# The 36 stores of bias rows of an attention and FFN kernel, issued by GpSimd in place of SyncE

## The chip, the cores and the metric

The kernel runs on one core of one Trainium2 chip. The metric is the device time of one execution in microseconds (us); the comparison below is between medians of several executions. Engines are named as the profile names them: PE (TensorE), DVE (VectorE), ACT (ScalarE), POOL (GpSimd) and SP (SyncE). SP does no arithmetic here: it only issues DMA transfers.

## The reference

Attention over 2 batches, 8 heads, 576 positions and 64 dimensions per head, with a position bias that a small network computes, followed by two feed-forward layers over the 1152 tokens:

```python
scores = scale * np.matmul(q, k.transpose(0, 1, 3, 2))
psi_rel = np.log1p(np.abs(pos[:, None] - pos[None, :]).astype(np.float32))
x = (psi_rel / np.log1p(np.maximum(pos[:, None].astype(np.float32), 1.0)))[..., None]
bias = np.maximum(x @ w1 + b1, 0.0) @ w2          # hidden 32, one column per head
attn = softmax(scores + bias.transpose(2, 0, 1)[None])
x = (attn @ v)                                     # to 1152 x 512
h = x @ w_in; x = (h * np.clip(h + 3.0, 0.0, 6.0) / 6.0) @ w_out     # d_ff 2048
xn = x / sqrt(mean(x * x) + 1e-06) * rms_g
out = (silu(xn @ w_gate) * (xn @ w_val)) @ w_out2  # d_ff 1536
```

## The kernel before

**Bias.** The bias is computed in 36 groups of 16 query positions (n = 0 to 35). For each group DVE and ACT build four tiles `R` (L361, L356), PE multiplies them with the second layer's weights into PSUM (`bias_mm`, rows `bps` L374, in the table B.n), ACT or DVE scales the result into a tile `ev` (`bias_evac`, L398 and L396; the pool has four such buffers, so group n+4 in issue order can only be written when the store of its predecessor in that buffer has landed), and `bias_store` (L404) writes it to DRAM: 16 positions x 8 heads x 591 values, in which the relative distances stand in one row. Eight groups make one DRAM buffer `biasd` (five of them, c = 0 to 4; the program calls c = 0, 1, 2, 3, 4 biasd_72, 73, 74, 75, 76). When all stores of a buffer have landed, `bias_load` (L427, L430) reads it back with a skewed pitch, so that each of 128 query rows gets its own 576 columns: tile `bias`, two heads at a time. The first unit's load is cut into its two heads.

**Attention.** It runs over 9 tiles of 128 queries and, in each, 4 pairs of heads: 36 units u. In a unit PE makes the scores `s` (S.u, L445), DVE adds the bias and takes the minimum into `e` (L458, twice, once per head), ACT takes the exponential (L469), PE transposes (T.u.0 to 2, rows `tps`), ACT or DVE copies to `et` (L489), and PE multiplies with v (PV.u, L507). q and k are transposed by PE first (qT, kT, rows `qps` and `kps`) and copied (`kS`, L332 on DVE; `q`, L342 on ACT). PE's order is a table written by hand, which contains among others `B.8 kT.0,0,1 qT.1.0 S.1 T.0.0 B.14 T.0.2 S.2`. The PSUM pool of the transposes has three buffers, that of the scores two. The loads of q (`rawq`, L290), k (`rawk`, L300) and v (`vs`, `v`, L308 and L310) and of the weights (`raw`, L127) are all issued by SP.

**Order.** Only PE's order is fixed by hand there. The other engines, SP among them, get their order when the program is built, from a scheduler with its own estimates; each engine then works strictly in that order. A DMA's semaphore is one of eight of its issuing side in turn, so a ninth DMA waits until the first of the eight has landed.

**POOL** does little in the attention part: the 1/sum rows are spread over a tile (`rb`, L521, which PE transposes as `rps`) and the lower half of the output is split off (`xl`, L543), each once for a tile. In the two feed-forward layers POOL makes the lower parts of the weights (`wl`, L168).

Of the kernel before, what the change touches and what calls it, by code (L numbers as in the profile page):

```python
# [65 lines left out]
def kernel(ctx, tc, q, k, v, w1, b1, w2, w_in, w_out, w_gate, w_val, w_out2, rms_g, dtab, ntab, itab, out):  # L66
    nc = tc.nc
    B, H, S, D = q.shape
# [170 lines left out]
    if True:  # L239
# [123 lines left out]
        ev_t = {}  # L363
# [36 lines left out]
        def bias_store(n):  # L400
            c, m = divmod(n, 8)
            dst = biasd[c][:(128 if c < 4 else 64) * (H + 1) * W].rearrange("(s h w) -> s h w", h=H + 1, w=W)
            lo = S - 16 - 16 * n
            nc.sync.dma_start(out=dst[16 * m:16 * m + 16, :H, lo:lo + S + 15], in_=ev_t.pop(n))  # L404

        def bias_rows(c, p):
            rows = 128 if c < 4 else 64
# [186 lines left out]
        for i, n in enumerate(n for c in order for n in range(8 * c, min(8 * c + 8, NG))):  # L594
            g = group_key(i)
            z = "z" if i < 8 else ""
            R_eng[n] = "".join(sorted(START[i] if i < 8 else MID[i % len(MID)], key="PDA".index))
            for j, x in enumerate(sorted(range(4), key=lambda x: "PAD".index(R_eng[n][x]))):
                e = R_eng[n][x]
                at(g + (P[z + "rp"] if e == "P" else P[z + "ra"] if e == "A" else P[z + "rd"] * j), ("R", n, x), (), bias_R, n, x, e)  # L600
            at(g + P[z + "b"], ("B", n), [("R", n, x) for x in range(4)] + [("cc",)], bias_mm, n)
            o = 16 * n + 15
            for h, length in enumerate((o, S - o)):
                e = "D" if length <= P[z + "evd"] else "A"
                at(g + P[z + "ev"] + .001 * h, ("EV", n, h), [("B", n)], bias_evac, n, h, e)
            key = g + P[z + "ev"] + .001 + P[z + "st"]
            at(key, ("ST", n), [("EV", n, 0), ("EV", n, 1)], bias_store, n)
            c = n // 8
            stored_key[c] = max(stored_key.get(c, -99), key)
# [335 lines left out]
```

## Time and profile before

| what | value |
|---|---|
| median of 3 runs | 646.74 us (646.6 to 648.12) |
| profiled execution, its own time | 646.28 us |
| span of its profile | 644.5 us |
| mean granted TensorE clock | 0.999 |
| PE busy | 622.3 us, 97% of the span |
| DVE, ACT, POOL busy | 461.5, 346.5, 144.5 us |

The span goes from the first to the last instruction; the profiled execution's own time lies 1.8 us above it. A busy share is a share of the whole span, and says little of one stage.

### The profile page before, as it was taken

What the parts mean: (1) busy time and instruction counts of PE and PEld (TensorE: products, weight loads), DVE (VectorE), ACT (ScalarE), POOL (GpSimd) and SP (SyncE); (2) the same over time, 40 slices, a digit from 0 to 9 for tenths busy, and PEclk for the clock granted to TensorE, in tenths of its full rate; (3) what the DMA queues carried; (4) which work ended last, traced back from release to release, by engine and by line L of the source; (5) the groups of instructions that cost most, each with busy time, mean ns of one, the idle gap of its engine ahead of it and who ended that gap; (6) DMA issues with size and microseconds to landing.
All of it is one profiled execution on the core that took longest, in us unless ns stands there. A gap on an engine that the chain in (4) does not pass through costs nothing.

```text
span 644.5 us, 10984 instructions
## 1 busy us (share of the span) xinstructions
PE 622.3 (97%) x4174; PEld 527.5 (82%) x4174; DVE 461.5 (72%) x855; ACT 346.5 (54%) x700; POOL 144.5 (22%) x116
## 2 busy tenths in 40 slices
PE   5889999998999999999999999999999999999997
PEld 2356666676788999999999989999899999999996
DVE  6797788647754999998833799969776761397812
ACT  4878676877765555555534556564444431253511
POOL 1000111011310333333310023323332340032400
PEclk9999999999999999999999999999999999999999
DMA  6999647478600344444310133443434350154301
GB/s 149 289 314 284 174 134 196 112 157 255 200 1 2 95 136 131 131 132 130 119 44 1 35 98 131 134 128 99 148 113 131 102 159 2 34 184 143 99 0 50
DMA packets 74721, 80.16 MB, mean 124 GB/s; under 512 B 23980, under 2 KB 59436, under 8 KB 74668
## 3 DMA queue, kind: packets, MB, share of 16 engines
q1 hardware_dynamic: 74668, 79.46, 41.8%
q8 instruction: 33, 0.54, 0.4%
q14 instruction: 20, 0.16, 0.1%
HBM read 66.19 MB, written 13.25 MB: 123 GB/s over the span
## 4 chain that ended last, share of the span: by engine, by line
PE 88%; DVE 4%; ACT 3%; DMA 3%; issue 1%; SPq 0%; DVEq 0%; ACTq 0%
PE h L735 39%; PE ya L780 18%; PE yb L780 9%; PE pv L507 6%; PE tps L103 5%; PE s L445 5%; PE bps L374 3%; DVE R L361 1%; ACT e L469 1%; ACT ev L398 1%; DMA raw<-in_moe_w_in_dram 1%; DVE e L458 1%; DMA bias<-biasd 1%; PE qps L103 1%; DMA biasd<-ev 1%
## 5 line engine op out<-in xcount | busy, mean ns | idle before, releaser
L168 POOL TENSOR_TENSOR wl<-wm,wh 128x512 fp32r<-128x512 f32 x85 | 126.3, 1486 | 302.4 <-ACT wh L139 183.3
L160 DVE SCALAR_TENSOR_TENSOR wm<-raw,wm 128x512 int32<-128x512 int32 x85 | 121.9, 1434 | 1.0
L744 ACT CAST gh<-r 128x384 fp32r<-128x384 f32 x84 | 43.2, 514 | 115.4 <-DVE r L767 68.6
L735 PE MATMUL h<-nh,wh 128*128 128x384 f32 x288 | 97.3, 338 | 0.0
L735 PE MATMUL h<-nh,wl 128*128 128x384 f32 x288 | 96.7, 336 | 0.0
L735 PE MATMUL h<-nl,wh 128*128 128x384 f32 x288 | 96.4, 335 | 0.0
L469 ACT ACTIVATE e<-e,m 128x576 f32<-128x576 f32 x72 | 55.5, 772 | 31.9 <-DVE m L458 31.7
L735 PE MATMUL h<-xh,wh 128*128 128x384 f32 x192 | 65.4, 341 | 0.0
L767 DVE TENSOR_TENSOR r<-r,h 128x384 f32<-128x384 f32 x36 | 19.9, 553 | 63.0 <-PE h L735 63.0
L735 PE MATMUL h<-xh,wl 128*128 128x384 f32 x192 | 64.7, 337 | 0.0
L735 PE MATMUL h<-xl,wh 128*128 128x384 f32 x192 | 64.4, 336 | 0.0
L156 DVE SCALAR_TENSOR_TENSOR wm<-raw,wm 128x512 int32<-128x512 int32 x85 | 59.4, 698 | 2.8
L458 DVE CUSTOM_DVE_ANT_1 e<-s,bias 128x576 f32<-128x576 f32 x72 | 52.4, 757 | 10.6 <-PE s L445 8.0
L147 ACT ACTIVATE wm<-raw 128x512 f32<-128x512 f32 x85 | 57.2, 673 | 3.5 <-DMA raw<-in_moe_w_in_dram 2.1
L747 DVE TENSOR_TENSOR gl<-r,gh 128x384 fp32r<-128x384 f32 x84 | 46.6, 554 | 16.8 <-ACT gh L744 16.8
L735 PEld LDWEIGHTS h<-nh,wh 128*128 128x128 f32 x288 | 54.1, 188 | 2.3 <-DVE nl L844 0.9
L735 PEld LDWEIGHTS h<-nl,wh 128*128 128x128 f32 x288 | 54.1, 188 | 1.4
L103 PE MATMUL tps<-ident,e 128*128 128x128 f32 x324 | 53.1, 297 | 2.0 <-ACT et L489 1.6
L361 DVE TENSOR_SCALAR R<-T,NB 128x320 f32<-128x320 f32 (+17 forms) x124 | 50.6, 462 | 6.0 <-PE bps L374 5.7
L735 PEld LDWEIGHTS h<-nh,wl 128*128 128x128 f32 x288 | 54.0, 188 | 0.0
L103 PEld LDWEIGHTS tps<-ident,e 128*128 128x128 f32 x324 | 41.5, 201 | 14.6 <-issue 7.3
L755 ACT ACTIVATE r<-h,half_c 128x384 f32<-128x384 f32 x48 | 27.7, 578 | 47.7 <-PE h L735 47.6
(102 smaller groups left out, 1095.8 us busy)
## 6 DMA issues: line engine op xcount, KB each, us to landing
raw<-in_moe_w_out_dram SPq DMA_DIRECT2D x33, 512.0 KB, 3.6
biasd<-ev SPq DMA_DIRECT2D x36, 295.5 KB, 3.7
raw<-in_moe_w_in_dram SPq DMA_DIRECT2D x18, 512.0 KB, 3.6
raw<-in_moe_w_gate_dram SPq DMA_DIRECT2D x18, 512.0 KB, 3.5
bias<-biasd SPq DMA_DIRECT2D x15, 576.0 KB, 4.8
raw<-in_moe_w_val_dram SPq DMA_DIRECT2D x16, 512.0 KB, 3.6
rawq<-in_q_dram SPq DMA_DIRECT2D x32, 128.0 KB, 4.6
bias<-biasd SPq DMA_DIRECT2D x10, 288.0 KB, 4.4
```

Source lines behind the costliest of these rows:

```text
L103: nc.tensor.transpose(out, in_, ident[:n, :n])
L147: nc.scalar.activation(out=m, in_=raw[:, :, 1].bitcast(F32), func=ACTF.Abs, scale=2.0 ** -112)
L156: nc.vector.scalar_tensor_tensor(out=m, in0=raw[:, :, 0], scalar=29, in1=m, op0=ALU.logical_shift_right, op1=ALU.bitwise_or,)
L160: nc.vector.scalar_tensor_tensor(out=m, in0=raw[:, :, 1], scalar=-0x80000000, in1=m, op0=ALU.bitwise_and, op1=ALU.bitwise_or,)
L168: nc.gpsimd.tensor_tensor(out=lo, in0=m, in1=hi, op=ALU.subtract)
L361: nc.vector.tensor_scalar(out=R, in0=src, scalar1=NB1[:, col], scalar2=None, op0=ALU.max)
L458: nc.vector.tensor_tensor_reduce(out=e_t[u][:, a, :].rearrange("p (j r) -> p r j", r=2), in0=s[:, :, :SH], in1=bt[u][:, a, :].rearrange("p ...
L469: nc.scalar.activation(out=e_t[u][:, a, :], in_=e_t[u][:, a, :], func=ACTF.Exp, scale=-1.0, bias=m_t[t][:, h:h + 1], accum_out=sum_t[t][:, ...
L735: nc.tensor.matmul(ps, lhsT=w[wz][:, c * 128:(c + 1) * 128], rhs=x[xz][:, c, :], start=(i == 0), stop=(i == 11),)
L744: nc.scalar.copy(out=gh, in_=g)
L747: nc.vector.tensor_tensor(out=gl, in0=g, in1=gh, op=ALU.subtract)
L780: nc.tensor.matmul(y_t[ph, n, t], lhsT=g[gz][:, t * 128:(t + 1) * 128], rhs=w[wz], start=(f == 0 and i == 0), stop=(f == F - 1 and i == 2),)
```

## The change

The stores of `bias_store` are issued on POOL's queue in place of SP's. Size, source and destination of the 36 transfers stay the same.

```diff
         def bias_store(n):
...
-            nc.sync.dma_start(out=dst[16 * m:16 * m + 16, :H, lo:lo + S + 15], in_=ev_t.pop(n))
+            nc.gpsimd.dma_start(out=dst[16 * m:16 * m + 16, :H, lo:lo + S + 15], in_=ev_t.pop(n))
```

The scheduler also gives three engines another order. The first place is SP's queue in the first part of the program, from the second pair of k loads on; `vs_140` and `v_142` are v of the first batch, `vs_141` of the second, and `bias<-biasd_74` are the first loads of bias rows (128x576: one head of unit 0; 128x2x576: a unit). Before:

```order
L404 DMA biasd_74<-ev 16x8x591 x2
L404 DMA biasd_73<-ev 16x8x591 x2
L430 DMA bias<-biasd_74 128x576 x2
L430 DMA bias<-biasd_74 128x2x576
L300 DMA rawk<-in_k_dram 128x4x128
L430 DMA bias<-biasd_74 128x2x576 x2
L404 DMA biasd_73<-ev 16x8x591 x3
L300 DMA rawk<-in_k_dram 128x4x128
L290 DMA rawq<-in_q_dram 128x4x64 x2
...
L308 DMA vs_140<-in_v_dram 128x4x128 x2
```

Now:

```order
L300 DMA rawk<-in_k_dram 128x4x128
L290 DMA rawq<-in_q_dram 128x4x64 x2
L308 DMA vs_140<-in_v_dram 128x4x128 x2
L310 DMA v_142<-in_v_dram 64x4x64
L308 DMA vs_140<-in_v_dram 128x4x128 x2
L310 DMA v_142<-in_v_dram 64x4x64
L308 DMA vs_141<-in_v_dram 128x4x128 x2
L430 DMA bias<-biasd_74 128x576 x2
```

Six of the eight `vs` loads, two of the four `v` loads and one more pair of `rawq` loads now stand ahead of the first bias load; they stood behind it.

The second place is DVE's order where the first two `e` of the attention stand (e_433, heads 0 and 1 of unit 0); kps_488 and kps_503 are transposed k blocks in two of PSUM's three buffers, R_533 and R_541 belong to group 14.

```order
 L361 TENSOR_SCALAR R_425<-T_113,NB1_116 128x448
-L361 TENSOR_SCALAR R_533<-T_113,NB1_116 128x352
-L361 TENSOR_SCALAR R_541<-T_113,NB1_116 128x352
-L332 COPY kS0_138<-kps_488 128x4x128
 L458 ISA e_433,m_435<-s_427,bias_394 128x2x288
 L458 ISA m_435 128x1
 L458 ISA e_433,m_435<-s_430,bias_394 128x2x288
 L458 ISA m_435 128x1
+L332 COPY kS0_138<-kps_488 128x4x128
+L361 TENSOR_SCALAR R_533<-T_113,NB1_116 128x352
 L332 COPY kS0_138<-kps_503 128x4x128
+L361 TENSOR_SCALAR R_541<-T_113,NB1_116 128x352
```

The copy of kps_488, which stood ahead of the two `e`, now stands behind both.

The third place is POOL's queue, from the last of its start-up work on; `rb` and `xl` are the per-tile rows named above.

```order
 L311 MEMSET v_143 64x4x64
+L404 DMA biasd_74<-ev 16x8x591 x8
+L404 DMA biasd_73<-ev 16x8x591 x8
+L404 DMA biasd_75<-ev 16x8x591
 L521 COPY rb<-ri 128x512
+L404 DMA biasd_75<-ev 16x8x591 x4
 L543 TENSOR_TENSOR xl_80<-xf,xh_77 128x4x128
 L521 COPY rb<-ri 128x512
```

The stores stand in POOL's order between its per-tile operations, in the order of the groups. PE's order is the same in both programs.

## Rows read from the trace of the kernel before

**Rows 1.** The page's busy times by engine, whole span.

```profile
PE 622.3 (97%) x4174; PEld 527.5 (82%) x4174; DVE 461.5 (72%) x855; ACT 346.5 (54%) x700; POOL 144.5 (22%) x116
```

**Rows 2.** Busy time by stretch; the last three columns are clock, DMA share, GB/s.

```profile
10.00:14.00 4.00, 4.00 (x32) 1.57 (x28) 3.51 (x12) 3.19 (x7) 0.00 (x0) 1.00 0.56 93
14.00:32.00 18.00, 15.25 (x124) 5.89 (x116) 13.59 (x38) 16.15 (x33) 0.00 (x0) 1.00 0.96 286
22.00:24.00 2.00, 1.05 (x16) 0.16 (x5) 2.00 (x7) 0.95 (x3) 0.00 (x0) 1.00 1.04 345
36.00:38.00 2.00, 1.75 (x12) 0.97 (x8) 2.00 (x7) 0.56 (x3) 0.00 (x0) 1.00 1.04 404
40.00:60.00 20.00, 19.46 (x184) 12.75 (x186) 16.60 (x44) 15.56 (x36) 0.61 (x1) 1.00 1.04 265
```

**Rows 3.** Chain of work that ended last, 20 to 34 us: start, us, what.

```profile
22.03 4.18 DMA biasd<-ev
...
26.78 5.23 DMA bias<-biasd
```

**Rows 4.** Timeline of PE, DVE and ACT, 16 to 37 us: start, us, [idle before <-releaser].

```profile
16.20 10.13 DVE L361 TENSOR_SCALAR R<-T,NB 128x368 f32<-128x368 f32 x29
...
23.20 2.06 ACT L398 ACTIVATE ev<-bps,cc,INV 128x224 f32<-128x224 f32 x4 [1.05 <-PE bps L374]
...
28.50 0.69 DVE L332 COPY kS<-kps 128x512 f32<-128x512 f32 x1 [2.17 <-PE kps L103]
...
29.98 0.76 DVE L458 CUSTOM_DVE_ANT_1 e<-s,bias 128x576 f32<-128x576 f32 x1 [0.78 <-DMA bias<-biasd]
...
30.06 0.60 PE L103 MATMUL qps<-ident,rawq 128*128 128x128 f32 x4
...
32.03 0.76 DVE L458 CUSTOM_DVE_ANT_1 e<-s,bias 128x576 f32<-128x576 f32 x1 [1.29 <-DMA bias<-biasd]
...
33.54 0.74 PE L103 MATMUL tps<-ident,e 128*128 128x128 f32 x4
...
35.20 1.24 PE L445 MATMUL s<-kS,q 64*128 64x288 f32 x8
```

**Rows 5.** Timeline of SP's DMA issues, 16 to 47 us.

```profile
16.73 1.23 SPq L300 DMA_DIRECT2D rawk<-in_k_dram  x2
...
26.37 1.36 SPq L430 DMA_DIRECT2D bias<-biasd  x3
...
33.55 3.23 SPq L290 DMA_DIRECT2D rawq<-in_q_dram  x2
...
39.79 1.19 SPq L308 DMA_DIRECT2D vs<-in_v_dram  x2
```

**Rows 6.** DMA issues, whole span: count, KB each, median us from issue to landing.

```profile
biasd<-ev SPq DMA_DIRECT2D x36, 295.5 KB, 3.7
...
rawq<-in_q_dram SPq DMA_DIRECT2D x32, 128.0 KB, 4.6
bias<-biasd SPq DMA_DIRECT2D x10, 288.0 KB, 4.4
rawk<-in_k_dram SPq DMA_DIRECT2D x8, 256.0 KB, 4.4
vs<-in_v_dram SPq DMA_DIRECT2D x8, 256.0 KB, 5.1
...
v<-in_v_dram SPq DMA_DIRECT2D x4, 64.0 KB, 4.9
```

**Rows 7.** DMA issues of 24 to 26 us, then of 30 to 32.4 us.

```profile
biasd<-ev SPq DMA_DIRECT2D x2, 295.5 KB, 3.3
...
biasd<-ev SPq DMA_DIRECT2D x3, 295.5 KB, 8.1
```

**Rows 8.** Timeline, 47 to 66 us: POOL's first operations and who meets them.

```profile
47.22 0.61 POOL L521 COPY rb<-ri 128x512 f32<-128x512 f32 x1 [38.63 <-DVE ri L516]
...
57.47 0.63 PE L103 MATMUL rps<-ident,rb 128*128 128x128 f32 x4 [0.29 <-ACT et L489]
...
64.04 1.89 DVE L361 TENSOR_SCALAR R<-T,NB 128x512 f32<-128x512 f32 x2
64.21 1.44 POOL L543 TENSOR_TENSOR xl<-xf,xh 128x512 fp32r<-128x512 f32 x1 [16.38 <-DVE xh L545]
```

**Rows 9.** What SP's queue waited for, whole span: us in total, times, longest.

```profile
SPq L404 <- ACT ev L398: 14.6, 10, 5.0
...
SPq L404 <- DVE ev L396: 10.4, 4, 7.2
```

## The prediction

> **What bounds the kernel now.** I read the page's busy times first: PE is busy 97% of the span [rows 1], so after the start any moment that PE stands still is paid in full. Then the busy time by stretch, to see where it stands still. From 14 to 32 us it works 15.25 of 18 us, from 40 to 60 us already 19.46 of 20 [rows 2]. So the start is where a change of queues can cost or give something; behind it only 0.54 us per 20 us is left to win. The chain of waits names what holds the start: the last of the eight stores of buffer c = 2 is issued at 22.03 and takes 4.18 us to land, then the second bias load is issued at 26.78 and takes 5.23 [rows 3]. The reader sees the other end of it in the timeline: DVE's first `e` waited 0.78 us for bias rows, its second 1.29 us, and started at 32.03 [rows 4].
>
> The same stretch shows the resource under it. The DMA engines are busy at a share of 0.96 from 14 to 32 us, at 286 GB/s, while from 10 to 14 us they have room (0.56) [rows 2]. A transfer then waits for what was issued ahead of it: two stores issued into a short queue (24 to 26 us) took 3.3 us to land, three issued behind bias loads (30 to 32.4 us) took 8.1 [rows 7]. So when the first bias rows land is a matter of how many bytes stand ahead of them.
>
> **The change part by part.** *The stores leave SP's queue.* SP spent 14.6 us in 10 waits for ACT's `ev` and 10.4 us in 4 waits for DVE's, standing at a store [rows 9]; these waits end. Who gains? What stands behind on SP: k, q and v loads, none of which anyone waited for at that place (k copies waited for PE, not for a DMA, `qps` has no wait at all [rows 4]). I put the gain at 0.
>
> *What SP does with the freedom* is the main term. Without stores to wait for, it runs ahead to loads that wait for nothing. In the order now, six `vs`, two `v` and two more `rawq` loads come before the first bias load; before, the `rawq` pair went out at 33.55 and `vs` from 39.79 on, when unit 0 had its bias already [rows 5]. Bytes that must move after 14 us before both heads of unit 0 have their bias, with sizes from [rows 6] (1 KB = 1024 bytes):
> - 7 stores of c = 2 (the first moves before 14): 7 x 0.303 = 2.12 MB
> - 2 `rawk` loads (the first of the three, at 16.73 and later before [rows 5], now moves in the room before 14): 0.52 MB
> - 4 `rawq`: 0.52 MB
> - 6 `vs` and 2 `v`: 1.57 + 0.13 = 1.70 MB
> - the bias rows themselves, 2 x 288 KB: 0.59 MB
> - 3 to 5 stores of the next buffer, which POOL issues as soon as their `ev` is there, beside SP's loads: 0.91 to 1.51 MB.
>
> That is 6.4 to 7.0 MB, at 286 GB/s 22.3 to 24.4 us from 14 us on, and about 1 us from the last byte to the semaphore (an estimate: the 3.3 us of [rows 7] less 1.1 us for 0.303 MB at 286 GB/s, half of it behind the data). The second head's rows land at 37.3 to 39.4 us; I take 38.4 against the 32.0 of before (26.78 + 5.23): **+6.4 us**. Bounds: at 345 GB/s, the best stretch with k loads and stores mixed [rows 2], 6.4 MB take 18.6 us: 33.6 us, or +1.6; at 265 GB/s, the stretch in which v and q were loaded [rows 2], 7.0 MB take 26.4 us: 41.4 us, or +9.4.
>
> *DVE's new order* adds to it. The copy of kps_488 now stands behind both `e` of unit 0, and qT.1.0 needs its PSUM buffer, and S.1 stands behind qT.1.0 on PE. Before, the copy (28.50) and `qps` (30.06) were done while the bias rows were under way [rows 4]. From the end of the second `e` to the end of S.2 it took before 36.44 - 32.79 = 3.65 us. Now this stretch holds the copy 0.69, `qps` 0.60, S.1 as long as S.2, 1.24, and then the same row of PE work from T.0.0 to S.2, 36.44 - 33.54 = 2.90: 5.43 us, so **+1.8 us**. DVE's own row (copy, two to four `R`, third and fourth `e`) ends at about 4.7 us of these, beside it. Bounds: 0 if later gaps of PE take it back, 1.8 if none; after 40 us there are few gaps, so I take 1.8.
>
> *What POOL pays.* The trace has no DMA issued by POOL. Below, one costs what SP's row shows, 0.5 us; above, take the 1.44 us of POOL's `xl` [rows 8]. At the low end POOL keeps pace with ACT, which makes two `ev` pairs in 2.06 us [rows 4]; at the high end the eighth store is late by up to 8 x 0.4 = 3.2 us. Both lie beside the loads' bytes, which have to move in either case: 0, with the 3.2 us partly in the upper end. Queued behind the waiting stores on POOL are `rb` and `xl`; `rb` was made at 47.22 and used by `rps` at 57.47 [rows 8], so 10 us of cover. There are 8 POOL operations of this kind under 140 us, all with stores of the same time beside them: 0.
>
> *A lock between DVE and POOL* is visible: while `xl` ran, two `R` took 1.89 us [rows 8], where 29 in a row took 10.13, 0.35 each [rows 4]; over 1 us lost by DVE. If issuing a store does the same, the 20 or so later stores cost DVE up to 1 us each. DVE is not what PE waits for in most of that time; I take 0, and 2 us for the upper end.
>
> Sum, against the profiled execution's own 646.28 us: 646.28 + 6.4 + 1.8 = **654.5 us**. That execution is 0.46 us below the median of the runs, well inside what the runs differ by.
>
> **The rivals.**
> - *The engines move faster with two queues* (650 us). If loads and stores side by side reach the 345 GB/s of the mixed stretch, the rows land at 33.6: +1.6, and with +1.8 the time is 649.7. For it: the fastest 2 us of [rows 2] reached 404 GB/s. Against it: that was with rows of stores and bias, and where v and q were loaded the rate was 265.
> - *DVE keeps POOL from writing its descriptors* (657.5 us). DVE runs 29 `R` without a gap from 16.20 to 26.33 [rows 4]. If POOL's stores can't start beside them, as `R` and `xl` did not run side by side [rows 8], the fourth store starts at 26.3 and lands 3.3 us later, at 29.6. The eighth group's `ev` needs the fourth's buffer (the 1.05 us that ACT stood before 23.20 ended when such a store landed), so its store goes out at about 31.5 and lands by 35. The second bias load is issued 0.6 later and takes 5.23 as before: 40.9, +8.9, and with +1.8 and some lost DVE time 657 to 659. The Trainium skill ("SBUF — State Buffer", the trap ahead of "A bandwidth-pool intuition that's wrong") says that a DMA issued from GpSimd gets its descriptors written by GpSimd's cores, which are shut out while VectorE runs an operation in a two-port mode. By that rule this rival is the case; the trace agrees that the two engines exclude each other, and has no row of a store.
> - *Not slower* (645 to 648 us). Stores on a queue of their own land without waiting for loads (3.3 in place of 4.18 us), SP is at the bias load in time, and the two waits of 0.78 and 1.29 us shrink: at best 646.28 - 1.3 = 645. It decides when the second head lands by 32.0 - 1.8 = 30.2 us, so that 6.4 MB would have to move in 15.2 us, 421 GB/s, above the fastest 2 us of the trace (404). Or the `vs` loads are held up on SP by something that I don't see, and stay behind the bias rows.
>
> **How the numbers follow.** The forecast (rows land at 36 to 40 us, 652 to 657) has 0.60, the faster engines (649 to 652) 0.15, DVE shutting out POOL (657 to 660) 0.13, not slower 0.12. The range 649.5 to 659.5 leaves out the last and the edges. A measurement of this kernel tells about 0.3%, 1.9 us, from no change. Of not slower I give 0.05 to faster and 0.07 to the same; the others are slower, 0.88.
>
> **What would show it.** In the profile after: the first `vs` issues stand before 25 us; the DMA share is about 1 from 14 us to the landing of the bias rows at 37 to 39 us; the first `e` of DVE waits several us for `bias<-biasd`; PE's busy share from 24 to 40 us falls by about 8 us; `qps` and S.1 come behind both `e`; from there on the profile of before is seen shifted by about 8 us, and the feed-forward part takes as long as before. It would be wrong if `vs` is issued early and the bias rows still land by 32 us (DMA not the limit), if PE makes up the delay between 40 and 200 us, or if the later stores slow DVE so much that PE waits for it there.

## The result and the profile after

The change made the kernel slower by 0.9%: 653.24 us (median of 4 runs, 651.84 to 655.32) against 647.43 us (median of 4, 646.6 to 648.81), ratio 1.0094 with an interval of 1.0077 to 1.0112. Run once more it took 653.32 us (median of 6, 652.67 to 654.92), ratio 1.0089 (1.0069 to 1.0109). The profiled execution of the first was the slowest of its four, 655.32 us and 9.0 us above the profiled one of before; that of the second took 652.86 us.

The page's busy times after, as in [rows 1]: PE works 5.5 us longer than before at the same number of matmuls, POOL 20.2 us longer for its 36 stores (0.56 us each).

```profile
PE 627.8 (96%) x4174; PEld 529.5 (81%) x4174; DVE 462.3 (71%) x855; ACT 347.1 (53%) x700; POOL 164.7 (25%) x152
```

The windows after, to compare with [rows 2] (the last three columns are the granted clock, the DMA share and GB/s):

```profile
14.00:32.00 18.00, 14.41 (x102) 4.96 (x95) 11.55 (x33) 12.74 (x25) 5.51 (x11) 0.88 1.02 283
32.00:40.00 8.00, 3.60 (x16) 1.34 (x15) 1.70 (x5) 2.47 (x6) 1.02 (x2) 0.50 1.00 336
40.00:60.00 20.00, 19.06 (x152) 12.17 (x152) 18.53 (x49) 15.48 (x35) 2.92 (x5) 0.88 0.92 251
```

From 14 to 40 us the DMA engines have no room left, at 283 GB/s up to 32 us, about the 286 that were expected, and PE works 3.60 of the 8 us from 32 to 40. New is the clock column: 0.50 from 32 to 40 us, the 1.2 GHz level, where every stretch of [rows 2] shows 1.00.

SP's DMA issues after, against [rows 5]; the DMA issues of the page, against [rows 6]:

```profile
18.25 2.38 SPq L308 DMA_DIRECT2D vs<-in_v_dram  x2
...
27.80 2.40 SPq L308 DMA_DIRECT2D vs<-in_v_dram  x2
30.52 2.79 SPq L430 DMA_DIRECT2D bias<-biasd  x3
```

```profile
biasd<-ev POOLq DMA_DIRECT2D x36, 295.5 KB, 3.9
...
vs<-in_v_dram SPq DMA_DIRECT2D x8, 256.0 KB, 8.1
```

The first `vs` goes out at 18.25 in place of 39.79, the first bias load at 30.52 in place of 26.37. The `vs` loads, now in the crowd, take 8.1 in place of 5.1. Over the whole span the stores land as fast as before (3.9 us, before 3.7), but not in this stretch. The eighth and last store of c = 2, for which the first bias load waits, goes out at 23.74 in place of 22.03 and takes 6.6 us where it took 4.18 [rows 3], as the DMA issues from 23.75 to 24.2 us show:

```profile
biasd<-ev POOLq DMA_DIRECT2D x1, 295.5 KB, 6.6
```

The chain of waits in that stretch, against [rows 3], and the timeline of DVE and PE, against [rows 4]:

```profile
23.74 0.53 POOL biasd L404
...
27.22 3.31 DMA biasd<-ev
30.52 7.76 DMA bias<-biasd
...
40.47 1.11 PE qps L103 x4
41.58 2.22 PE s L445 x8
```

```profile
38.30 0.76 DVE L458 CUSTOM_DVE_ANT_1 e<-s,bias 128x576 f32<-128x576 f32 x1 [12.37 <-DMA bias<-biasd]
...
39.04 0.76 DVE L458 CUSTOM_DVE_ANT_1 e<-s,bias 128x576 f32<-128x576 f32 x1
...
39.72 0.69 DVE L332 COPY kS<-kps 128x512 f32<-128x512 f32 x1
...
40.47 1.11 PE L103 MATMUL qps<-ident,rawq 128*128 128x128 f32 x4 [3.03 <-DVE kS L332]
...
41.51 2.29 PE L445 MATMUL s<-kS,q 64*128 64x288 f32 x8
```

The chain names the store issued at 27.22 for the wait that ended at 30.52. By its place in POOL's queue that one is the ninth, of the next buffer; what ended the wait is the eighth, whose 6.6 us end at 30.4. So both are late in the crowd: the store that the bias load waits for, and the bias load itself (7.76 us; before, the second one took 5.23).

DVE's first `e` waits 12.37 us for bias rows where it waited 0.78; the second starts at 39.04 in place of 32.03. Behind both come the copy, `qps` and S.1, as DVE's new order has it, and each matmul at half the clock: `qps` 1.11 us (0.60 before), S.1 2.29 (1.24).

The second profile of the same kernel shows how much executions differ:

```profile
36.02 0.76 DVE L458 CUSTOM_DVE_ANT_1 e<-s,bias 128x576 f32<-128x576 f32 x1 [10.08 <-DMA bias<-biasd]
...
36.75 0.76 DVE L458 CUSTOM_DVE_ANT_1 e<-s,bias 128x576 f32<-128x576 f32 x1
...
38.76 1.76 PE L445 MATMUL s<-kS,q 64*128 64x288 f32 x8
```

The second `e` starts at 36.75 here. Two marks serve for all runs below: the start of the second `e`, when the bias rows of unit 0 are complete, and that of PV.0, PE's first `pv`. Before, PV.0 started here:

```profile
47.70 1.09 PE L507 MATMUL pv<-et,vs 128*64 128x128 f32 x16
```

| kernel | second `e` | PV.0 | whole profiled time |
|---|---|---|---|
| before | 32.03 | 47.70 | 646.28 |
| after, first profile | 39.04 (+7.0) | 56.79 (+9.1) | 655.32 (+9.0) |
| after, second profile | 36.75 (+4.7) | 54.07 (+6.4) | 652.86 (+6.6) |

All of the loss is there when PV.0 starts, and next to none is won back in the 597 us behind it.

### The profile page after: what moved, and what is told of

It is laid out like the page before. It is cut to its first block, busy times and chain, and to the rows that moved or that the text cites. A ratio compares the mean times of both kernels' runs of the same rounds, so it can differ in the third digit from the quotient of the medians.

```text
span 653.5 us, 11014 instructions
## 1 busy us (share of the span) xinstructions
PE 627.8 (96%) x4174; PEld 529.5 (81%) x4174; DVE 462.3 (71%) x855; ACT 347.1 (53%) x700; POOL 164.7 (25%) x152
## 4 chain that ended last, share of the span: by engine, by line
PE 85%; DVE 5%; DMA 4%; ACT 3%; issue 2%; SPq 0%; POOL 0%; ACTq 0%; DVEq 0%; POOLq 0%
PE h L735 39%; PE ya L780 18%; PE yb L780 9%; PE pv L507 5%; PE tps L103 5%; PE s L445 5%; PE bps L374 3%; DVE e L458 1%; DMA biasd<-ev 1%; DMA bias<-biasd 1%; DVE R L361 1%; ACT e L469 1%; PE qps L103 1%; ACT ev L398 1%; DMA raw<-in_moe_w_in_dram 1%
## 5 line engine op out<-in xcount | busy, mean ns | idle before, releaser
L139 ACT CAST wh<-wm 128x512 fp32r<-128x512 f32 x85 | 52.4, 617 | 1.3 <-DVE wm L160 1.1
L755 ACT ACTIVATE r<-h,half_c 128x384 f32<-128x384 f32 x48 | 27.8, 579 | 47.7 <-PE h L735 47.6
```

Of the source, the lines that this page charges most:

```text
L139: nc.scalar.copy(out=hi, in_=m)
```

## The experiments

**1. The loads put back.** In the changed kernel, v and the early pair of q loads are queued on SP behind the bias load of unit 3 (`held`).

```diff
-                    nc.sync.dma_start(out=a, in_=q[b, h, ...
+                    with tc.issue_after(held["bias", 3]) if (t, hh) == (1, 1) else ExitStack(): nc.sync.dma_start(out=a, in_=q[b, h, ...
...
-                    nc.sync.dma_start(out=vs[b][:, blk, o::2]...
+                    with tc.issue_after(held["bias", 3]): nc.sync.dma_start(out=vs[b][:, blk, o::2]...
```

> The changed kernel, stores on POOL, but the loads of v and the early pair of rawq loads queued on SP behind the first bias loads; PE, DVE, ACT and POOL keep the changed kernel's order row for row. If the bytes of those loads ahead of the bias rows are the cause (my theory), the second head's rows land at 30 to 33 us in place of 39.0, TensorE keeps its full clock through the wait, and what is left of the slowdown is at most the 1.8 us of DVE's new order: 0 to +2 us against the kernel before, ratio 1.000 to 1.003. If issuing on POOL or two queues at once is the cause (rival), the rows still land after 36 us and the time stays 5 to 6 us above before, ratio 1.008 or more.

Measured: 649.32 us, ratio 1.0034 (1.0019 to 1.0048). Its timeline:

```profile
32.34 0.76 DVE L458 CUSTOM_DVE_ANT_1 e<-s,bias 128x576 f32<-128x576 f32 x1
...
34.35 2.29 PE L445 MATMUL s<-kS,q 64*128 64x288 f32 x8
```

The rows are back (32.34), and of the ratio's 0.0094 some 0.0060 or 3.9 us are gone. What I expected of the clock was wrong (S.1 still takes 2.29 us), and 0.0034 or 2.2 us stay.

**2. Part of those bytes ahead, without POOL.** The kernel before with all stores on SP; the v loads of the first batch get an earlier key (the number that sets their place) in the plan, and SP's order changes in nothing but their place, ahead of the last two stores of c = 2. (DVE gets six `R` ahead of the copy and both `e` as well, which fall into the wait.)

```diff
-lv0=0.532, lv1=1.209
+lv0=-1.5, lv1=1.209
```

> The kernel before, all stores on SP, but only the four vs and two v loads of the first batch (1.18 MB) ahead of the last two stores of c = 2; no rawq or rawk load changes its place. A smaller dose of the same suspect, without the rawq load that the run with all of v moved. If bytes ahead of the bias rows are the cause: 1.18 MB at 286 GB/s is 4.1 us, the second head's rows land at 35.5 to 37 us in place of 32.0, and the time is 3 to 5 us above before, ratio 1.005 to 1.008. If they cost only together with POOL's queue: ratio 1.001 or less.

Measured: 651.22 us, ratio 1.0065 (1.0042 to 1.0088).

```profile
34.80 0.78 DVE L458 CUSTOM_DVE_ANT_1 e<-s,bias 128x576 f32<-128x576 f32 x1
```

The second `e` is late by 2.8 us (expected 3.5 to 5) and the time by 3.6 (4.2 by the ratio; expected 3 to 5). PV.0 starts at 51.62 in this profile, 3.9 us later than before, of 3.8 us in all. The loads hold up the last two stores of c = 2 on SP, which go out at 26.0 at the latest in place of 22.03 [rows 3]. The clock was at 0.67 from 32 to 36 us, so a part of the price can be the clock's. So loads ahead of the bias rows cost without any change of queues.

**3. All of v ahead, without POOL.** As above, with both batches early.

```diff
-lv0=0.532, lv1=1.209
+lv0=-1.5, lv1=-1.499
```

> The kernel before, all stores on SP and POOL issuing nothing, but the eight vs and four v loads ahead of the last two stores of c = 2 and so of the first bias loads (their place in the plan's keys moved from 0.53 and 1.21 to -1.5). This puts the suspected cost in without the suspected queue. If bytes ahead of the bias rows are the cause: 2.36 MB more, less 0.13 MB of a rawq load that moves behind, at 286 GB/s 7.8 us: the second head's rows land at 38 to 40 us in place of 32.0, and the time is 5 to 9 us above before, ratio 1.008 to 1.014. If POOL's queue is the cause: ratio 1.002 or less.

Measured: 665.51 us, ratio 1.0288 (1.0266 to 1.0310), twice what was expected at most. The timeline and the chain:

```profile
39.91 0.76 DVE L458 CUSTOM_DVE_ANT_1 e<-s,bias 128x576 f32<-128x576 f32 x1
```

```profile
42.99 7.55 DMA rawq<-in_q_dram
...
50.67 1.09 PE qps L103 x4
```

The bias rows came as expected: the second `e` started at 39.91. But then PE waited for the q load that had moved behind: issued at 42.99, landed at 50.54, and `qps` and S.1 could only come then. The run confirms the landing and says nothing on the price of it; the smaller dose above does.

**4. DVE's order alone.** In the kernel before, the copy of kps_488 queued behind both `e` of unit 0.

```diff
-            copy(engine)(out=dst, in_=src)
+            with tc.issue_after(held[0, 1].ins) if x == (0, 1, 1) else ExitStack(): copy(engine)(out=dst, in_=src)
```

> The kernel before, stores on SP, but the copy of the first k block in question (kps_488) queued on DVE behind both e of unit 0, as the changed kernel has it; PE's and SP's orders are those of before. If the term for DVE's order was right: the stretch from the end of the second e to the end of S.2 is 5.4 us in place of 3.65, and the time +1.8 us, ratio 1.003. If PE takes it back in gaps that it has anyway: the stretch is longer but the time within 0.5 us of before, ratio 0.999 to 1.001.

Measured: 647.02 us, ratio 1.0001 (0.9985 to 1.0017). But it didn't test what it should: `qps` here waited for ACT's `ev` and not for the copy, so it must have been given another of the three PSUM buffers, and it started before the second `e` had ended (31.75 to 32.51).

```profile
31.70 0.66 PE L103 MATMUL qps<-ident,rawq 128*128 128x128 f32 x4 [0.67 <-ACT ev L398]
```

**5. The loads and DVE's order put back.** As the first run, and the first two `e` queued behind the copy.

```diff
-            copy(engine)(out=dst, in_=src)
+            y = copy(engine)(out=dst, in_=src).ins; x == (0, 1, 1) and [tc.add_manual_dep(held[0, i].ins, y.name, ...) for i in range(2)]
```

> The kernel with v and q loads behind the bias loads and stores on POOL, and also the copy of kps_488 ahead of both e of unit 0 on DVE, as before the change. If bytes and DVE's order are the whole story: nothing of the slowdown is left, ratio 0.998 to 1.001, and the stretch from the second e to the end of S.2 is 3.7 us again; a ratio below 0.998 would say that stores on a queue of their own gain something once SP's order is kept. If POOL's queue costs: ratio 1.006 or more.

Measured: 649.64 us, ratio 1.0040 (1.0028 to 1.0052): no better than with the loads alone. Its timeline:

```profile
33.32 0.75 DVE L458 CUSTOM_DVE_ANT_1 e<-s,bias 128x576 f32<-128x576 f32 x1
...
36.70 1.24 PE L445 MATMUL s<-kS,q 64*128 64x288 f32 x8
...
40.08 0.76 DVE L458 CUSTOM_DVE_ANT_1 e<-s,bias 128x576 f32<-128x576 f32 x1 [1.33 <-DMA bias<-biasd]
...
42.27 0.76 PE L103 MATMUL kps<-ident,rawk 128*128 128x128 f32 x4 [2.72 <-ACT et L489]
```

From the end of the second `e` (34.07) to the end of S.2 (37.94) it is 3.87 us, so the order does what was said of it in its own stretch. But then the `e` of unit 2 waits for its bias rows until 40.08 (before it started at 37.01), and PE stands 2.72 us behind it. In this execution the 1.8 us are not paid out, since the next thing is late: bias rows of later units.

**6. Who delays the later bias rows.** Only the eight stores of c = 2 on SP, the other 28 on POOL, loads put back.

```diff
-            nc.sync.dma_start(out=dst[16 * m:16 * m + 16, ...
+            (nc.gpsimd if c != 2 else nc.sync).dma_start(out=dst[16 * m:16 * m + 16, ...
```

> The eight stores of c = 2, for which the first bias loads wait, stay on SP; the other 28 go on POOL; v loads and the early rawq pair are queued on SP behind the bias loads, and DVE has the order of before up to the sixth e. The stores of the next buffer (c = 1) then no longer stand behind the bias loads of units 1 to 3 in one queue. If their competition with those loads is what was left of the slowdown when the loads were put back (2.3 to 2.6 us there): the second head's rows land by 32.5 us, but PE waits 2 to 3 us for later bias rows between 34 and 43 us, ratio 1.003 to 1.005. If the first eight stores on POOL are what was left: ratio 0.999 to 1.001.

Measured: 649.56 us, ratio 1.0027 (1.0016 to 1.0038). The second `e` of unit 0 and the first of units 1 and 2 in its timeline, then those of units 1 and 2 in the kernel before:

```profile
32.19 0.76 DVE L458 CUSTOM_DVE_ANT_1 e<-s,bias 128x576 f32<-128x576 f32 x1 [0.38 <-DMA bias<-biasd]
...
35.73 0.76 DVE L458 CUSTOM_DVE_ANT_1 e<-s,bias 128x576 f32<-128x576 f32 x1 [1.55 <-DMA bias<-biasd]
...
39.40 0.76 DVE L458 CUSTOM_DVE_ANT_1 e<-s,bias 128x576 f32<-128x576 f32 x1 [0.51 <-DMA bias<-biasd]
```

```profile
33.94 0.75 DVE L458 CUSTOM_DVE_ANT_1 e<-s,bias 128x576 f32<-128x576 f32 x1
...
37.01 0.75 DVE L458 CUSTOM_DVE_ANT_1 e<-s,bias 128x576 f32<-128x576 f32 x1
```

Unit 0 is on time, unit 1 late by 1.8 us and unit 2 by 2.4, both waiting for bias rows. About 0.6 us of either is there when the loads go out (the first at 26.98, before at 26.37). On one queue two stores of the next buffer went ahead of the first bias load and the other six stood behind the loads of units 0 to 3 (the first three of them are those of 30 to 32.4 us in [rows 7]). On POOL's queue they go out between these loads:

```profile
27.86 0.43 SPq L430 DMA_DIRECT2D bias<-biasd  x1
...
28.63 0.53 POOL L404 DMA_DIRECT2D biasd<-ev  x1 [0.45 <-ACT ev L398]
...
29.50 2.86 SPq L430 DMA_DIRECT2D bias<-biasd  x2
```

So they run beside them, with the DMA engines at a share of 0.97 from 28 to 32 us and 1.02 from 32 to 36. The twenty later stores, which this run has on POOL as well, are not what costs in this profile: PV.0 starts at 49.77, 2.1 us later than before, of 2.0 us in all, and the first of the twenty goes out at 48.75. Nor is it the clock, which was 1.00 from 24 to 48 us. The Trainium skill ("DMA: Bandwidth & Descriptors", "Queues, rings and completion order") says that an engine takes turns between the queues, a packet from each; these waits agree with it, though no run here shows the turns themselves.

**7. The later stores alone.** Only the last 20 stores on POOL, from 48 us on.

```diff
-            nc.sync.dma_start(out=dst[16 * m:16 * m + 16, ...
+            (nc.gpsimd if c not in (1, 2) else nc.sync).dma_start(out=dst[16 * m:16 * m + 16, ...
```

> Only the last 20 stores (c = 3, 4, 0, from 50 us on) on POOL, the first 16 on SP; PE's and DVE's orders are those of before. If the change costs only in the start: within 0.6 us of before, ratio 0.999 to 1.001. If stores beside DVE's work cost DVE or PE time later on, or if freeing SP of them gains anything there: off by 1 us or more, ratio above 1.0015 or below 0.9985.

Measured: 648.85 us, ratio 1.0025 (1.0010 to 1.0041), more than I expected. But in its profile PV.0 starts at 49.06, 1.36 us later than before, of an excess of 1.9 in all, and POOL issues its first store at 48.1. A window says why:

```profile
38.00:44.00 6.00, 4.96 (x26) 2.84 (x27) 4.10 (x10) 4.51 (x11) 0.00 (x0) 0.72 1.07 271
```

The clock was at 0.72 here where the profile of before has 1.00, with POOL idle (the column before the clock) and SP, DVE and ACT in the order of before. That part is the execution's, not the change's; whether the rest is, these runs do not settle. By measured time alone this run (0.0025) and the one before it (0.0027) can't be told apart; it is the profile of that one that puts its excess at the bias rows.

**8. The clock kept up.** The changed kernel with eight extra matmuls (`fill`) in PE's waits, whose result nobody reads; DVE's `R` of two groups are queued later (not shown).

```diff
+            ps_of["k", x] = turn_four(raw_t["k", *x], "kps"); fill({(0, 1, 1): 2, (0, 0, 1): 4}.get(x, 0))
...
+            ps_of["b", n] = ps; fill(2 if n == 11 else 0)
```

> The changed kernel with eight extra 512-column matmuls on PE whose result nobody reads, two behind group 11, two behind kT.0,1,1 and four behind kT.0,0,1, where PE waits in the changed kernel; DVE's R of groups 15 and 24 are queued behind the third and fourth e. If the lost clock is on the path: the granted clock stays at 1.00 from 24 to 46 us, S.1 takes 1.24 us in place of 2.29, and the time is 2 to 3 us below the changed kernel's, about 650.5 us, ratio to before 1.004 to 1.006. If the half clock only fills time that PE waits anyway: the clock stays up but the time stays within 0.7 us of the changed kernel's 653.2, ratio to before 1.008 to 1.010.

Measured: 653.95 us, ratio 1.0108 (1.0089 to 1.0127). The clock stayed up, but SP's order had changed too:

```profile
53.76 0.63 PE L103 MATMUL kps<-ident,rawk 128*128 128x128 f32 x4 [1.07 <-DMA rawk<-in_k_dram]
```

So once more, with the last `rawk` load ahead of the four `rawq` again:

```diff
-                    nc.sync.dma_start(out=a, in_=q[b, h, ...
+                    with tc.issue_after(held["k", 1, 1, 1]) if t == 2 else ExitStack(): nc.sync.dma_start(out=a, in_=q[b, h, ...
```

> The changed kernel with the same eight extra matmuls as in the run with filled waits, whose result nobody reads, and on SP the last rawk load ahead of the four rawq loads again, since in that run PE waited 1.07 us for it and lost what the full clock had given. If the lost clock is on the path: granted clock 1.00 throughout, no wait for rawk, and a time 1.5 to 2.5 us below the changed kernel's, ratio to before 1.006 to 1.007. If PE gives it back in waits for other engines: ratio 1.009 to 1.011 as in that run.

Measured: 652.89 us, ratio 1.0081 (1.0064 to 1.0099), against 1.0089 of the changed kernel itself. Its windows and timeline:

```profile
24.00:48.00 24.00, 20.32 (x114) 9.35 (x111) 12.23 (x33) 14.71 (x31) 4.01 (x8) 1.00 1.07 342
```

```profile
38.25 0.76 DVE L458 CUSTOM_DVE_ANT_1 e<-s,bias 128x576 f32<-128x576 f32 x1 [2.38 <-DMA bias<-biasd]
...
40.26 1.24 PE L445 MATMUL s<-kS,q 64*128 64x288 f32 x8
...
43.09 1.24 PE L445 MATMUL s<-kS,q 64*128 64x288 f32 x8
...
46.54 0.66 PE L103 MATMUL kps<-ident,rawk 128*128 128x128 f32 x4 [0.66 <-DVE kS L332]
```

With the full clock the stretch from the second `e` (ends 39.01) to the end of S.2 (44.33) takes 5.32 us, against 7.25 in the first profile (39.80 to 47.05). PE then waits 0.66 us for DVE and shorter for ACT, and the time as measured is the same. The lost clock is real, but keeping it up returned nothing that these runs can tell from noise (0.0081 against 0.0089 and 0.0094), so it is not the main cost.

**9. The changed kernel again.**

> The changed kernel as it is, once more, since its ratio so far rests on few runs and its profiled execution had the lowest clock of them. My theory: ratio 1.008 to 1.011 again; if the profile is of an execution with a clock of 0.99 or more, the bias rows still land at 38 to 39.5 us and its time is 1 to 3 us below the 655.3 of the first profile, since S.1 and its neighbours are then shorter. If the clock is what costs (rival): the time follows the clock, and an execution near 0.995 is within 2 us of before.

Measured: 653.32 us, as told above. Its profile had a mean clock of 0.994 and was 2.5 us below the first, but only partly by the clock: the bias rows came 2.3 us earlier (36.75 against 39.04). That they land at 38 to 39.5 whatever the execution was wrong; and at 0.994 it was still 6.6 us above before, so the rival is wrong too.

No version tried here beats the kernel before.

## Why the prediction was right, step by step

- **Bytes ahead of the bias rows, +6.4 us: the mechanism is right, the size about two thirds.** The rows were forecast for 38.4 us and came at 39.0 and 36.7. The rate, 283 GB/s from 14 to 32 us, is the 286 that was used. What the sum did not say is that the bytes also delay the stores for which the bias load waits: the eighth took 6.6 us to land, with the loads put back 3.1. (It also went out 1.7 us later than before, but so it did, at 24.04, with the loads put back.) Put back, the loads returned about 3.9 us, and a part of them moved ahead alone cost 3.6 us (4.2 by the ratio). In time the term is nearer 4 than 6.4, each to within about 1 us. One reason shows in the timelines of the first run and of the changed kernel, at the third `e`:

```profile
36.28 0.76 DVE L458 CUSTOM_DVE_ANT_1 e<-s,bias 128x576 f32<-128x576 f32 x1 [0.73 <-DMA bias<-biasd]
```

```profile
42.89 0.76 DVE L458 CUSTOM_DVE_ANT_1 e<-s,bias 128x576 f32<-128x576 f32 x1 [0.63 <-PE s L445]
```

  With the loads put back it waits for its own bias rows, in the changed kernel for PE's scores only. Once unit 0 is late, the later rows are no longer waited for.
- **DVE's order, +1.8 us: right in its stretch, not in the time.** 5.43 us were worked out, 5.32 measured at the full clock. But undoing it returned nothing, since the bias rows of unit 2 were late behind it. The step that failed is "0 if later gaps of PE take it back": I looked for gaps of PE further on, where the next transfer was late 4 us on.
- **What stands in its place** is a step the prediction did not have. I counted the stores of the next buffer as bytes ahead of unit 0's rows only. Freed from SP's order, they also run beside the bias loads of units 1 and 2 and delay them by 1.8 and 2.4 us; the run that has this and neither the early loads nor the new order was 1.8 us slower (0.0027 of 647.7). The sum of 3.9 and 1.8 is 5.7, where the two measurements give 6.1 and 5.8 by their ratios. With each term good to about 1 us, this leaves no large cost unnamed; it doesn't show that there is no smaller one. That the forecast of 8.2 us came out near is in part luck: one term was too large, one was not paid, and one was missing.
- **The signs.** They came as named but for one: PE's busy time from 24 to 40 us fell from 12.1 to 8.8 us, by 3.3 and not by about 8.
- **What POOL pays: right.** The store takes 0.53 us as on SP, the row of the tile `biasd`: duration in ns least, median and most.

```profile
L404 POOL DMA_DIRECT2D biasd<-ev x36: 532/532/732, 12.2 to 144.9; - x36
```

- **The rival that DVE shuts POOL out** was not the cause, but isn't wholly wrong. In the first profile the stores at 16.14, 18.25 and 19.23 took 0.73, 0.60 and 0.61 us in the midst of DVE's run of 23 `R` from 16.02 to 24.09:

```profile
16.02 8.07 DVE L361 TENSOR_SCALAR R<-T,NB 128x368 f32<-128x368 f32 x23
...
18.25 0.60 POOL L404 DMA_DIRECT2D biasd<-ev  x1 [1.37 <-ACT ev L398]
```

  (Such a row merges what follows closely; this one has pauses at 17.41 and 21.39, of 0.27 and 0.09 us, and the stores of 18.25 and 19.23 lie between them. The row of 29 `R` that the prediction read as without a gap has such pauses too, at 17.66 and 21.63, so that a store shut out by `R` would not have had to wait until 26.3, as the 657.5 us assume.) In the second profile, one store was held:

```profile
18.64 4.55 POOL L404 DMA_DIRECT2D biasd<-ev  x3 [1.60 <-ACT ev L398]
```

```profile
L404 POOL DMA_DIRECT2D biasd<-ev x36: 530/530/3327, 12.2 to 142.2; - x36
```

  The first of these three took 3.33 us and ended at 21.97, right behind a pause of DVE of 0.09 us (21.86 to 21.95). So it went in three of the six profiled executions that had such stores (once 2.12 us, twice 3.33). The rule of the Trainium skill that the prediction named ("SBUF — State Buffer") has GpSimd locked out while VectorE runs an operation in a two-port mode; the prediction took it to hold through a whole run of `R`. That one store waited for a pause in some executions agrees with it, that the others came through within 0.25 us of their usual time does not; no run here shows which mode `R` runs in. And the execution with the held store had its bias rows 2.3 us earlier than the one without, so the held store did not decide. There the `vs` loads ahead were all issued by 27.8 us, in the first profile by 30.2, which fits the loads as the cause.
- **The rival of faster engines** (rows at 33.6 us) did not come; 336 GB/s were reached from 32 to 40 us, too late. **Not slower** was refused by the first landing.
- **SP's freed waits, 0:** right; no run that freed SP was faster than before.
- **The profiled time** was forecast against 646.28, an execution at full clock; the forecast of 654.5 lies between the two profiles after (655.32 and 652.86) and 1.2 to 1.3 above the medians.

## What to carry to other kernels

Stores that wait on a queue also hold back the loads behind them; when they were taken off here, the scheduler filled the queue with loads for which nobody waited yet. Where the DMA engines are full, count the bytes that will stand ahead of the next transfer that is waited for, and also what will run beside the transfers after it. If the queues are split, order the loads that are not urgent behind the urgent ones explicitly.

## What the runs showed of the hardware that was not expected

- TensorE's granted clock fell to its 1.2 GHz level when PE had waited: in the first profile to 0.50 from 28 us on, after a wait of 2.10 us and with another of 3.03 us still ahead, and back to 1.00 by 46 us. Matmuls took up to 1.85 times as long (S.1 2.29 us against 1.24). It also fell in executions of kernels that did not have the long wait (0.72 from 38 to 44 us in the run of the later stores), and not in the profile of before. The eight filled matmuls kept it at 1.00.
- A store issued by POOL is held, in some executions, until DVE's run of `R` has a gap: 2.12 and 3.33 us against 0.53.
- The same program's bias rows landed 2.3 us apart in two executions, with the DMA engines full in both.
